# A hand-laid instruction order for attention plus feed-forward, with the list laid out anew: k of batch 0 loaded first, k of batch 1 behind v, 29 filler products

## Chip, core and metric

The kernel runs on one core of a Trainium2 chip. A core has TensorE (PE, which multiplies matrices), VectorE (DVE), ScalarE (ACT) and GpSimd (POOL) as computing engines, and SyncE (SP), which here only issues DMAs. Each engine runs its own list of instructions in order; semaphores make one list wait for another. The metric is the time of one execution on the device in microseconds (us); lower is better.

## The reference

Two parts, one behind the other. The first is block attention with sorted blocks: for 4 batches of 8 heads, 768 positions of 64 numbers are cut into 8 blocks of 96. A matrix `sort_net` of 8x8 per head is normalised five times over rows and columns, and the blocks of k and v are mixed by it.

```python
for _ in range(5):
    P = exp(P - max(P, axis=-1))
    P = P / sum(P, axis=-1)
    P = P / sum(P, axis=-2)
k_sorted = einsum('bhij,bhjcd->bhicd', P, k_blocks)
v_sorted = einsum('bhij,bhjcd->bhicd', P, v_blocks)
attn = softmax(scale * q_block @ k_sorted_block.T)
x = (attn @ v_sorted_block), heads side by side     # 3072 x 512
```

The second part is a feed-forward layer over the 3072 rows of x:

```python
h = x @ w_in                                        # 512 -> 2048
g = max(h, 0) + alpha * min(h, 0)
out = g @ w_out                                     # 2048 -> 512, float32
```

## The kernel before

The work goes by batch b (4) and within it by block (8), so by 32 groups g, each with the 8 heads of one block. For each group PE makes scores and softmax weights (products into the PSUM banks psS, psH), the products with v (psO, psYP), and transposes of the result into xT, which is the input of the feed-forward layer. That layer runs in chunks of groups: FFN1 (L875, w_in) writes psH, ACT and DVE turn psH into hT (L885, L889), FFN2 (L915, w_out) multiplies hT by w_out into psYP. The first chunks take 2 groups each, later ones 4.

Names that matter below:
- Loads. q, k and v of batch 0 come as three transfers of 768 KB, issued by POOL (L426 into hT, L449 into KS0 and VST0). The weights come in 4 (w_in, L960) and 2 (w_out, L965) transfers. Of the later batches k goes to KS1 and KS0 in turn (L449), v to VST1 and VST0 in two halves each (L465), q to QN, one transfer for each head (L431). All of these are issued on POOL's queue and their transfers land in the order of issue.
- `sinkhorn` (L548 to L562) is a chain of small steps on DVE and ACT; its last step gives Pb. PE spreads it over the partitions (L569), and DVE makes BDK from that (L573), the matrix that sorts k and v of batch 0.
- q of batch 0 is transposed by PE (L643) and copied into QTz0. k of batch 0 is sorted by PE (`prep_k`, L630) in six units and cast into KT0 by DVE or ACT (L401); one further copy, KT0<-KT0, fills a pad behind the first two units ("the pad copy"). v of batch 0 is copied into hT in eight units (hT<-VST, L401), sorted (L714) and copied into VS0.
- The matrices BDM and BDV, which sort k and v of batches 1 to 3, come from nine small PE products (L587, L590, "the spread"), two DVE products with mkj and mkjV and a sum dsel (L595, L600).
- For batches 1 to 3, KSz and VDz are padded copies of k and v (L655, L401) that PE multiplies (L668, L709).
- Scores are made twice: once turned, to find the row maximum nm (L759, L765), once for the exponentials (L781, L771). Group 1 is the first one. For g of 8 and more it is once (L756, nf).

What sets the order: nothing is planned at run time or at build time. `SEQ` (L32 to L79) is a table written as numbers. Each number is an operation of the program in the order in which `add` made it; a letter behind it picks the engine where there is a choice (p POOL, a ACT, d DVE; without a letter the first one allowed). `arrange` appends the operations to the five lists in the table's order, and `emit` puts a wait only where a list needs what another has made. An entry like `i15Y` stands for 15 filler products (L1047): identity times identity into a PSUM bank (Y is psYP, O psO, G psH), whose results nobody uses. PE runs them in its place in the list like all others. The kernel before has 42 of them: 22 ahead of the spread L569, 19 up to group 2's scores, one later.

Of the kernel before, what the change touches and what calls it, by code (L numbers as in the profile page):

```python
# [32 lines left out]
0 2 11 7 3 10 4 1 8 25 39 42 43 5 9 27 44 17 33 i1Y 45 i4Y 24 46 47 6 48 49 14 50 28 i2Y 51 52 53 i15Y 23 54  # L33
55 143 56 57 58 26 59 127 60 61 62 21 63 64 126 65 66 22 67 128 68 69 29 70 71 16 72 73 13 74 129 85 86 87 75
76 77 78 40 79 80 81 37 88 134 82 96 97d 94 91 92 98 38 89 130 12 144 95 90d i2Y 140 93a 83 84 100 i3Y 99d 20
136 101d 102d 105a 103d 154 i3Y 104 106 155 109 114 115 15 145 146 110 111 107d 112 113 i3Y 116 117d 147 108a
118 119d 148 122 123d 137 120 156 121 124 139 132 19 125d 135 233 133 157 i2Y 158 159 149 150 160d i3G 179 180
i1P 41 138 i2P 161 162d 151 152 18 181 30 35 36 34 153d 163 188 182 196 164 165 205 166 167p 197 189 190 191
232 206 183 230 184 207 192 193 185d 198 209 142 199 186 i1Y 231 237 210 141 194 195 221 208 131 187 213 200
211 212 222 244 214 201 223 215 216 248 245 224 249 202d 246 247 203 204d 250 251 217 225 258 218 236 226 262  # L40
263 219 220 234 241 235 227d 266 267 259 260 173 228 229 252 238 276 268 239 253 264 242 269 305 172 288d 170
174 240 280 261 279 286 243 270 315 265 289 290 277 278 271 287 293 294 306 307 272d 273 308 275 291 274 281
292 297 295 342 282d 298 283 309 284 296 301 302 285 316 343 317 310 299 344 300 328 311d 303 304 312 314 313d
320 326 332 32 321d 345 346 327 169p 333 324 329 347 325 353 348d 254 171p 349 334 335 175 354 255 256 350d
323 367 318 395 330 382 331 396 319d 392 336 351 393 383 384 397 394 419 416 420 322 352d 355 356 358d 31 365
398 399 337 366 357 338 408 421 409 359 257 425 417 400 418 426 422 339 428 360d 361 427 423 424 411 449 410
385 340 368 446 429 362 363 439 450 451 455 430 364d 447 448 369 176 458 459 414 443 456 415 386 387 388d 412
452 453 370 454 440 389 401 460 371 438 390d 402 476 488 457 479 413 403 404d 489 405 372 512 177 469 431 406d
432 477 178 441 461 480 444 478 482 442 481 485 433 434d 490 524 491 373 483 472 435 378 377 486 374 436 487
513 380 445 462 375 484 509 463 510 464d 470 379 471 506 507 381 511 465 466d 508 525 514 376 521 522 523 518  # L50
519 520 515 516d 526 527 492 517 474 545 475d 542 168 554 560 391 493 543 546 544 547 468 500 501 494d 555 548
473 561 549 550 502 437 495 496d 562 407 503d 551 552 556 499 577 553 563 578 579 498 504 505 533 528 529 557
558 589 530d 535 534 538 539 571 572 590 583 584 580 341 531 581 625 626 537 536 569 582 586 591 540 587 585
622 570d 541 573 574 575 532 600 576 627 588 623 631 598 624 599 564 632 559 628 629 565 601 634 566d 567 635
# [1035 lines left out]
```

## Time and profile before

| | us |
|---|---|
| median of 3 runs (lowest to highest) | 235.51 (235.39 to 235.55) |
| the profiled execution's own time | 235.32 |
| its span in the trace | 233.6 |
| DVE busy | 167.6 (72%) |
| ACT busy | 156.0 (67%) |
| POOL busy | 102.7 (44%) |

TensorE's granted clock is 1.00 in every stretch of the trace. Start times below are microseconds from the span's start; the own time of the execution is 1.7 us longer than its span.

How to read rows: in the timeline a row is a run of alike instructions: start, time from its first start to its last end, engine, line, operation, output<-input, size, count; in brackets idle time of that engine before it, and what ended it. In the windows view a row is a stretch of the span, with the busy time and count of PE, of PE's weight loads, of DVE, ACT and POOL, then the granted clock.

### The profile page before, as it was taken

The numbers are of one execution on the slowest core, as the hardware profiler recorded it, in microseconds if no ns is written. First come the engines' busy times: TensorE is split into PE (matmuls) and PEld (weight loads), VectorE is DVE, ScalarE is ACT, GpSimd is POOL, SyncE is SP. The second block draws the span as 40 slices with busy tenths as digits, with TensorE's granted clock in tenths as the row PEclk, the third lists the DMA queues.
The fourth block names the chain that finished last, engine by engine and source line by source line (L and its number), as shares of the span: only waits on it lengthen the run. The fifth ranks groups of instructions, "written<-read, shape, count | busy, mean of one in ns | idle before, by whom it ended". The sixth has DMA issues, their size and how long they took to land.

```text
span 233.6 us, 6277 instructions
## 1 busy us (share of the span) xinstructions
PE 225.4 (96%) x2528; PEld 140.4 (60%) x2556; DVE 167.6 (72%) x339; ACT 156.0 (67%) x417; POOL 102.7 (44%) x149
## 2 busy tenths in 40 slices
PE   6989999999999999999999999999999999999995
PEld 4356588795666666665566565555555555555653
DVE  5769799999878788586689668467787677544541
ACT  4187666989889678778888677766676674333431
POOL 7999139849049994863969953000000000000000
PEclk9999999999999999999999999999999999999999
DMA  5999999996996899869939997944643523410203
GB/s 66 220 206 204 218 200 185 186 182 99 218 189 106 115 152 174 196 102 225 192 63 164 137 103 164 154 90 79 130 107 74 112 51 109 124 45 0 94 0 135
DMA packets 73389, 31.36 MB, mean 134 GB/s; under 512 B 64512, under 2 KB 68368, under 8 KB 73360
## 3 DMA queue, kind: packets, MB, share of 16 engines
q0 software_dynamic: 24816, 13.63, 43.5%
q1 hardware_dynamic: 48544, 17.33, 37.2%
q8 instruction: 20, 0.33, 0.6%
q14 instruction: 9, 0.07, 0.1%
HBM read 27.28 MB, written 6.29 MB: 144 GB/s over the span
## 4 chain that ended last, share of the span: by engine, by line
PE 86%; DMA 4%; POOL 4%; DVE 3%; issue 2%; ACT 1%; POOLq 0%
PE psH L875 33%; PE psYP L915 28%; PE psYP L1047 4%; DMA VST<-in_v_dram 4%; PE psS L915 4%; PE psO L813 3%; PE psS L756 3%; POOL VDz L401 2%; PE psYP L668 2%; PE psYP L709 2%; PE psS L771 1%; PE psO L848 1%; DVE hT L401 1%; PE psS L781 1%; PE psO L915 1%
## 5 line engine op out<-in xcount | busy, mean ns | idle before, releaser
L889 DVE SCALAR_TENSOR_TENSOR hT<-t,omaT,psH 128x384 bf16<-128x384 f32 (+1 forms) x140 | 76.5, 568 | 37.4 <-ACT t L885 36.5
L875 PE MATMUL psH<-xT,w_in_bf 128*128 128x384 bf16 (+1 forms) x560 | 96.7, 310 | 0.6 <-DVE hT L889 0.6
L885 ACT ACTIVATE t<-psH 128x384 f32<-128x384 f32 x126 | 60.9, 493 | 44.5 <-PE psH L875 41.6
L915 PE MATMUL psYP<-w_out_bf,hT 128*128 128x512 bf16 x310 | 79.2, 379 | 1.4
L875 PEld LDWEIGHTS psH<-xT,w_in_bf 128*128 128x128 bf16 x560 | 50.0, 98 | 29.0 <-DVE hT L889 2.1
L915 PEld LDWEIGHTS psYP<-w_out_bf,hT 128*128 128x128 bf16 x336 | 30.8, 98 | 28.3 <-DVE hT L889 0.3
L793 ACT ACTIVATE Esb<-psS,nf 96x96 bf16<-96x96 f32 x192 | 46.1, 345 | 0.9 <-DVE nf L765 0.8
L401 POOL COPY VDz<-VST 64x384 bf16<-64x384 bf16 x40 | 34.5, 862 | 17.4 <-DMA VST<-in_v_dram 10.4
L655 POOL COPY KSz<-KS 64x512 bf16<-64x512 bf16 x36 | 22.0, 611 | 16.6 <-DMA KS<-in_k_dram 8.2
L765 DVE TENSOR_REDUCE nf<-psS 96x8 f32<-96x768 f32 x24 | 22.8, 950 | 6.4 <-PE psS L756 6.2
L826 DVE TENSOR_TENSOR xq<-psO,rec 96x512 bf16<-96x512 f32 x30 | 20.5, 684 | 0.7
L431 POOL DMA_DIRECT2D QN<-in_q_dram x24 | 19.9, 846 | 0.7 <-POOL QN L491 0.6
L401 ACT ACTIVATE outstg<-psYP 128x512 f32<-128x512 f32 x15 | 9.0, 601 | 7.7 <-PE psYP L915 7.5
L813 PEld LDWEIGHTS psO<-VS,ET 112*128 112x128 bf16 x248 | 11.1, 98 | 4.0 <-ACT xT L401 0.2
L1047 PE MATMUL psYP<-identb 128*128 128x512 bf16 x39 | 12.7, 470 | 0.8 <-ACT identb L401 0.8
L813 PE MATMUL psO<-VS,ET 112*128 112x65 bf16 x248 | 12.7, 194 | 0.0
L756 PEld LDWEIGHTS psS<-KT,QTz 128*128 128x128 bf16 (+1 forms) x192 | 10.7, 101 | 3.2 <-ACT KT L401 0.2
L401 ACT ACTIVATE VS<-psYP 112x512 bf16<-112x512 f32 x16 | 11.0, 688 | 2.1 <-PE psYP L714 1.1
L756 PE MATMUL psS<-KT,QTz 128*128 128x96 bf16 (+1 forms) x192 | 12.2, 207 | 0.0
L709 PEld LDWEIGHTS psYP<-BDV,VDz 128*128 128x128 bf16 x192 | 8.3, 98 | 3.0 <-POOL VDz L401 0.3
L401 ACT ACTIVATE KT<-psYP 128x512 bf16<-128x512 f32 x14 | 8.4, 600 | 2.2 <-PE psYP L668 2.0
L709 PE MATMUL psYP<-BDV,VDz 128*128 128x64 bf16 x192 | 9.5, 193 | 0.1
(140 smaller groups left out, 200.2 us busy)
## 6 DMA issues: line engine op xcount, KB each, us to landing
out_dram<-outstg SPq DMA_DIRECT2D x23, 256.0 KB, 2.5
KS<-in_k_dram POOLq DMA_DIRECT2D x3, 768.0 KB, 10.1
QN<-in_q_dram POOLq DMA_DIRECT2D x24, 96.0 KB, 4.5
w_in_bf<-in_moe_w_in_dram POOLq DMA_DIRECT2D x4, 512.0 KB, 16.8
w_out_bf<-in_moe_w_out_dram POOLq DMA_DIRECT2D x2, 1024.0 KB, 18.7
VST<-in_v_dram POOLq DMA_DIRECT2D x4, 384.0 KB, 11.1
hT<-in_q_dram POOLq DMA_DIRECT2D x1, 768.0 KB, 7.4
VST<-in_v_dram POOLq DMA_DIRECT2D x1, 768.0 KB, 12.8
```

Of the source, the lines that this page charges most:

```text
L401: return e.activation(o, i, ACTF.Copy) if e is nc.scalar else e.tensor_copy(o, i)
L655: G.add(POOL, lambda e, hp=hp: e.tensor_copy(AP(KSz, hp * 64 * 3072 + u % 3 * 1024 + hp * 64, [[3072, 64], [128, 8], [1, 64]]), AP(KS[n], ...
L709: inst = e.matmul(AP(t, off + dd * 64, [[row, 128], [1, 64]]), AP(VDz, (u % VSL * 8 + dd) * 128, [[VSL * 1024, 128], [1, 128]]), AP(BDV, b ...
L756: inst = e.matmul(o, AP(QTz[n], hp * 3072 + h4 * 768 + i * 96, [[6144, 128], [1, w]]), AP(KT[n], (h4 * 8 + i) * bk, [[ld, 128], [64, 2], [ ...
L765: G.add(DVE, lambda e: e.tensor_reduce(AP(nx, 0, [[8, 96], [4, 2], [1, 4]]), AP(psX, 0, [[1024, 96], [512, 2], [96, 4], [1, 96]]), AxisLis ...
L793: inst = e.activation(AP(Esb[me], p * 128, [[1024, 96], [64, 2], [1, 48]]), AP(psX, (p // 4) * 512 + (p % 4) * 96, [[1024, 96], [48, 2], [ ...
L813: inst = e.matmul(AP(psZ, hp * 512 + h4 * 68, [[1024, 128], [1, 65]]), AP(ET[me] if far else ET[m], pos(h4, hp) * 96, [[800, nk], [1, 128] ...
L875: inst = e.matmul(AP(pt, poff + x * n, [[1024, 128], [1, n]]), AP(w_in_bf, kt * DFF + (ft + x) * 128, [[KT_TILES * DFF, 128], [1, 128]]), ...
L885: G.add(ACT, lambda e: e.activation(AP(t1[tb], 0, [[384, 128], [1, k * n]]), AP(pt, poff, [[1024, 128], [1, k * n]]), ACTF.Relu, scale=-1. ...
L889: G.add(DVE, lambda e, x=x: e.scalar_tensor_tensor(out=AP(hT, (ft + x) * RING + tok % RING, [[FT_TILES * RING, 128], [1, n]]), in0=AP(t1[t ...
L915: inst = e.matmul(AP(bank[0], bank[1], [[1024, 128], [1, n]]), AP(hT, ft * RING + tok % RING, [[FT_TILES * RING, 128], [1, 128]]), AP(w_ou ...
L1047: inst = e.matmul(AP(t, off, [[1024, 128], [1, 512]]), identb[:, :], AP(identb, 0, [[128, 128], [0, 4], [1, 128]]))
```

## The change

Only `SEQ` differs; its text is one line shorter, so each line number behind it is one less in the changed kernel (L401 becomes L400, and so on). No operation other than fillers is added or removed. The first line of the table before and after:

```diff
-0 2 11 7 3 10 4 1 8 25 39 42 43 5 9 27 44 17 33 i1Y 45 i4Y 24 46 47 6 48 49 14 50 28 i2Y 51 52 53 i15Y 23 54
+0 10 1 7 5 2 3 8 39 4 42 43 44 45 12 11 35 46 47 48 49 6 50 16 51 40 13 52 9 27 53 i17Y 54 55 17 37 56 134 57
...
```

- Loads. POOL issued, with memsets between, q, k0, v0, half of v1, the four of w_in, k1, half of w_out, the other half of v1 and the eight QN transfers, the last five of these behind the hT copies. Now it issues k0, q, v0, k1, the four of w_in and one QN transfer, then makes its hT copies (which wait for v0), then issues half of w_out, a QN transfer, half of v1, and so on.
- Fillers. 29 instead of 42: 17 ahead of L569's spread, 8 ahead of group 1's scores, 4 behind the first product with v. The one after the first FFN1 groups and those between the scores and v's sorting are gone.
- FFN1 and FFN2. Eight FFN1 groups of 8 products (192 columns each) stand ahead of the first w_out product, where ten did.
- hT copies. POOL makes four and DVE two in a row (three and two before, and a third by DVE later); ACT makes the rest.

Three places are shown as rows of an engine's list.

The DVE list from BDK to the last step ahead of the first product with v (omaT is a small constant of the feed-forward layer, one0, mkj and mkjV masks), before:

```order
L573 TENSOR_TENSOR BDK<-mkh,psYP 128x128
L517 TENSOR_REDUCE one0<-identf 112x1
L401 CAST KT0<-psO 128x32x2x8
L401 CAST KT0<-psH 128x32x2x8
L401 CAST KT0<-psYP 128x32x2x8
L401 CAST KT0<-psH 128x32x2x8
L401 COPY hT<-VST0 128x8x48 x2
L765 TENSOR_REDUCE nm1<-psH 96x8
L765 TENSOR_REDUCE nm0<-psS 96x8
L401 COPY hT<-VST0 128x8x48
L401 CAST VS0<-psO 112x64x8 x4
L972 TENSOR_SCALAR omaT<-psYP 128x16
```

The same place of DVE's list after:

```order
L572 TENSOR_TENSOR BDK<-mkh,psYP 128x128
L505 TENSOR_REDUCE mkj<-identf 128x8
L400 COPY QTz0<-psO 128x768
L400 CAST KT0<-psYP 128x32x2x8
L400 CAST KT0<-psH 128x32x2x8
L400 CAST KT0<-psO 128x32x2x8
L400 COPY hT<-VST0 128x8x48 x2
L400 COPY KT0<-KT0 128x32x16
L764 TENSOR_REDUCE nm1<-psH 96x8
L400 CAST VS0<-psO 112x64x8
L764 TENSOR_REDUCE nm0<-psS 96x8
L400 CAST VS0<-psO 112x64x8
```

A copy of q into QTz0 has come from ACT to DVE and one cast of KT0 has gone to ACT; the pad copy KT0<-KT0 has come from ACT to DVE and stands behind the two hT copies, which wait for v0. Behind these rows DVE has one more cast of VS0 from psYP and one from psO, mkjV (which stood behind group 2's scores before) and omaT.

PE's list from the first product with v (L813, L812 after) to the third FFN1 group, before:

```order
L813 MATMUL psYP<-VS0,ET1 128x65 x8
L813 MATMUL psO<-VS0,ET0 128x65 x8
L1047 MATMUL psH<-identb 128x512 x3
L759 MATMUL psS<-KT0,QTz0 128x96 x8
L1047 MATMUL psYP<-identb 128x512 x3
L848 MATMUL psYP<-identb,xq1 128x96 x4
L848 MATMUL psO<-identb,xq0 128x96 x4
L781 MATMUL psS<-QTz0,KT0 128x96 x8
L771 MATMUL psS<-identb,nm0 128x96 x8
L587 MATMUL psYP<-Pb,selk 128x64 x3
L590 MATMUL psYP<-Pb,selk 64x64 x6
L875 MATMUL psH<-xT,w_in_bf 128x192 x8
```

After:

```order
L812 MATMUL psYP<-VS0,ET1 128x65 x8
L812 MATMUL psO<-VS0,ET0 128x65 x8
L1046 MATMUL psH<-identb 128x512 x4
L758 MATMUL psS<-KT0,QTz0 128x96 x8
L847 MATMUL psYP<-identb,xq1 128x96 x4
L847 MATMUL psO<-identb,xq0 128x96 x4
L780 MATMUL psS<-QTz0,KT0 128x96 x8
L770 MATMUL psS<-identb,nm0 128x96 x8
L874 MATMUL psH<-xT,w_in_bf 128x192 x8
L586 MATMUL psYP<-Pb,selk 128x64 x3
L589 MATMUL psYP<-Pb,selk 64x64 x6
```

The first FFN1 group has passed the nine products of the spread, and six fillers have become four.

POOL's list around the loads of batch 2 (KS0 and VST0 are free again by then), before:

```order
L401 COPY VDz<-VST1 64x8x48
L615 TENSOR_TENSOR BDV<-mkhV,dsel 128x64
L449 DMA KS0<-in_k_dram 128x3072
L401 COPY VDz<-VST1 64x8x48 x2
L504 MEMSET Esb1 96x16x16
L465 DMA VST0<-in_v_dram 64x3072 x2
L401 COPY VDz<-VST1 64x8x48
L401 COPY VDz<-VST0 64x8x48 x12
```

After:

```order
L400 COPY VDz<-VST1 64x8x48
L614 TENSOR_TENSOR BDV<-mkhV,dsel 128x64
L400 COPY VDz<-VST1 64x8x48 x3
L464 DMA VST0<-in_v_dram 64x3072
L400 COPY VDz<-VST1 64x8x48
L448 DMA KS0<-in_k_dram 128x3072
L464 DMA VST0<-in_v_dram 64x3072
L400 COPY VDz<-VST1 64x8x48 x2
L400 COPY VDz<-VST0 64x8x48 x4
```

The two halves of v2 and k2 are now issued behind the fifth and the sixth of POOL's VDz copies of batch 1; before, k2 was issued behind the fifth of eight and v2 behind the seventh.

More of the change, by code (lines that the diff above doesn't have):

```diff
@@ L32 @@
 SEQ = """
-0 2 11 7 3 10 4 1 8 25 39 42 43 5 9 27 44 17 33 i1Y 45 i4Y 24 46 47 6 48 49 14 50 28 i2Y 51 52 53 i15Y 23 54
[L34 to L52, printed above, removed]
```

70 lines of the change are left out of this document (44 added, 26 removed).

## The prediction, made before the changed kernel ran

> **What bounds the kernel now.** I read the page's head first.
>
> ```profile
> span 233.6 us, 6277 instructions
> ...
> PE 225.4 (96%) x2528; PEld 140.4 (60%) x2556; DVE 167.6 (72%) x339; ACT 156.0 (67%) x417; POOL 102.7 (44%) x149
> ```
>
> PE is busy for 96% of the span. But an average hides where the missing 8 us lie, so the second view is the table of stretches. I cut it at 28.7 us, where the first FFN1 group is about to start, and where the loads of batch 2 end.
>
> ```profile
> 28.70:54.80 26.10, 25.96 (x422) 21.21 (x423) 24.86 (x62) 20.78 (x37) 16.96 (x28) 1.00 1.40 178
> 54.80:73.00 18.20, 17.34 (x181) 10.88 (x182) 14.83 (x24) 15.96 (x49) 9.60 (x13) 1.00 0.99 178
> 73.00:92.00 19.00, 18.79 (x203) 12.09 (x206) 15.83 (x31) 14.66 (x44) 16.03 (x20) 1.00 1.15 132
> 92.00:231.00 139.00, 137.92 (x1108) 81.06 (x1123) 91.26 (x159) 88.19 (x254) 37.68 (x54) 1.00 0.61 111
> ```
>
> From 28.7 us on PE is full: 25.96 of 26.10, later 137.92 of 139.00. What a changed order can win there is only PE's waiting, most of it in the second row (0.86 us of 18.20). Ahead of 28.7 us PE runs fillers, and waits for loads and DVE. So the kernel is a **front** that ends when PE has enough to do, and a **body** with a fixed amount of PE work. The change does not touch that amount, apart from fillers. A microsecond in the front is a microsecond of the time, and so is each wait of PE in the body. DVE is the second engine to watch: 24.86 of 26.10 in the first stretch.
>
> The third view is the timeline of the front; the two rows in the last of these three fences are of the page's table of DMA issues (size, and us from issue to landing).
>
> ```profile
> 1.31 1.02 POOL L426 DMA_DIRECT2D hT<-in_q_dram  x1 [0.79 <-POOLq L1075]
> ...
> 4.12 0.55 POOL L449 DMA_DIRECT2D VST<-in_v_dram  x1
> ```
> ```profile
> 11.98 0.81 ACT L401 ACTIVATE QTz<-psO 128x768 bf16<-128x768 bf16 x1 [1.17 <-PE psO L643]
> ...
> 15.26 0.61 PE L1047 MATMUL psYP<-identb 128*128 128x512 bf16 x2
> ...
> 16.62 0.82 PE L1047 MATMUL psYP<-identb 128*128 128x512 bf16 x3
> ...
> 16.73 0.69 DVE L401 CAST KT<-psH 128x512 bf16<-128x512 f32 x1
> 17.08 3.09 POOL L401 COPY hT<-VST 128x384 bf16<-128x384 bf16 x3
> 17.34 2.10 DVE L401 COPY hT<-VST 128x384 bf16<-128x384 bf16 x2
> ...
> 17.61 0.35 PE L759 MATMUL psH<-KT,QTz 64*128 64x96 bf16 x8 [0.17 <-ACT QTz L401]
> ...
> 19.37 0.94 DVE L765 TENSOR_REDUCE nm<-psH 96x8 bf16<-96x768 f32 x1
> ...
> 21.10 0.58 DVE L401 COPY hT<-VST 128x384 bf16<-128x384 bf16 x1
> ...
> 25.00 0.42 PE L813 MATMUL psYP<-VS,ET 112*128 112x65 bf16 x8 [0.17 <-DVE omaT L972]
> ...
> 27.86 0.34 DVE L401 COPY xT<-psYP 128x384 bf16<-128x384 bf16 x1
> ...
> 28.33 0.37 DVE L509 TENSOR_REDUCE mkjV<-identf 128x8 f32<-128x128 f32 x1
> ```
> ```profile
> hT<-in_q_dram POOLq DMA_DIRECT2D x1, 768.0 KB, 7.4
> ...
> VST<-in_v_dram POOLq DMA_DIRECT2D x1, 768.0 KB, 12.8
> ```
>
> q lands at 1.31 + 7.4 = 8.7 us, v of batch 0 at 4.12 + 12.8 = 16.9. k lies between them, and the three are equally large, so one of them takes about 4.1 us and the second lands near 12.8. Group 1's scores (L759, 17.61) are early enough; DVE reaches the maximum nm only at 19.37, when its two hT copies are done. From nm to the first product with v (L813) it is 25.00 - 19.37 = 5.63 us of VS casts, exponentials and omaT.
>
> **The change part by part.** The sum is made against the profiled execution's own 235.32 us, 0.19 below the median shown (235.51); I carry the sum over as it is.
>
> Fillers: 13 fewer. Two take 0.61 us and three 0.82, so one more costs 0.21; were they on the path, 13 would be worth 13 x 0.21 = -2.7 us. I take 0, since what they stand in front of waits for transfers and DVE anyway: they fill time, and take it only where the awaited thing is there already. The granted clock is 1.00 in all stretches, and no run shows here what it would be with fewer.
>
> Front: k first, q second. q's transposes and copies move from 8.7 to behind 12.8; sorted k waits for BDK from the sinkhorn chain as before. The step that decides is DVE's list, by the rows quoted: a copy of q into QTz0 is now DVE's (ACT's took 0.81), then three casts of 0.69, then the two hT copies (2.10), then the **pad copy**, and only then can L759 run, since it reads KT0 with its pad. So: q at 12.8, transposes of 36 products (about 1 us) and waits, QTz copy 14.25 to 15.1; casts to 17.15; v has landed at 16.9, so nothing waits for it; hT copies to 19.25; pad copy to 20.05; L759's 0.35 to 20.4, and nm starts there. Before it started at 19.37: +1.03. Behind nm a DVE hT copy is gone (-0.58) and mkjV has come in (+0.37). The first product with v moves by 1.03 - 0.58 + 0.37 = **+0.8**, to about 25.8.
>
> The pad copy on DVE is in no row of before. Its nearest rows: a copy of the same kind of data alone, 0.34 (27.86); the hT copies of DVE beside POOL's, 2.10 / 2 = 1.05 against 0.58 alone (21.10), so +0.47 for the company. POOL will be in the midst of its four hT copies (1.03 each by the row at 17.08), so I take 0.34 + 0.47 = 0.8; with the largest surcharge of a row (+0.72, below) it is 1.06. The ends of this term: pad copy 0.34 and hT copies at 0.58 each give -0.6; 1.06 gives +1.1.
>
> Spread behind the first FFN1 group: PE's first useful FFN work is earlier by the nine small products, but DVE gets its two L595 products and dsel behind them later, while it is nearly full (24.86 of 26.10, so 1.24 idle). Lower end 0, if the idle time covers it; upper end +1.1, if nearly all that idle time opens anew in front. DVE's list loses work in this stretch to ACT (a KT1 cast, a VDz copy of 0.57, BDV), which speaks for the lower half: I take **+0.4**.
>
> Batch 2's loads earlier, and VDz copies moved: the two waits of PE in the body.
>
> ```profile
> 54.65 1.29 DVE L401 COPY VDz<-VST 64x384 bf16<-64x384 bf16 x1
> ...
> 57.63 1.47 PE L875 MATMUL psH<-xT,w_in_bf 128*128 128x384 bf16 x8 [0.57 <-DVE hT L889]
> ...
> 58.73 0.57 DVE L401 COPY VDz<-VST 64x384 bf16<-64x384 bf16 x1
> ```
> ```profile
> 66.99 10.88 POOL L401 COPY VDz<-VST 64x384 bf16<-64x384 bf16 x12 [8.11 <-DMA VST<-in_v_dram]
> ```
> ```profile
> 54.81 0.50 PE L756 MATMUL psS<-KT,QTz 128*128 128x96 bf16 x8
> 55.15 0.81 PE L875 MATMUL psH<-xT,w_in_bf 128*128 128x384 bf16 x4
> ```
> ```profile
> 68.12 0.52 PE L756 MATMUL psS<-KT,QTz 128*96 128x96 bf16 x8
> 68.77 0.41 PE L709 MATMUL psYP<-BDV,VDz 128*128 128x64 bf16 x8
> ```
>
> At 57.63 PE has stood for 0.57 us because DVE was late with hT, and DVE was late because a VDz copy beside POOL's copies took 1.29 instead of 0.57 (+0.72); that copy now stands earlier in DVE's list. At 68.12 a run of L756 keeps PE 0.65 us to the next start instead of 55.15 - 54.81 = 0.34, because L709 needs VDz of batch 2, whose data landed shortly before 66.99: POOL had stood 8.11 us for it. Its loads are now issued behind the fifth and sixth copy instead of the seventh, and the KSz and VDz copies themselves stand earlier, so the landing comes some microseconds sooner and 0.31 goes. Together **-0.9**. Lower end of the gain: 0, if another wait follows in each place; what is late next is the scores' exponentials on ACT, which was 15.96 of 18.20 busy.
>
> Sum: 235.32 + 0.8 + 0.4 - 0.9 = 235.6 us, rounded to the tenth. With all ends added up: 235.32 - 0.6 - 0.9 = 233.8, and 235.32 + 1.1 + 1.1 = 237.5.
>
> Here a rule bears on the pad copy. The Trainium skill, "SBUF — State Buffer", section "Who interferes with whom", says that DVE in a 2-port mode and GpSimd share one pair of ports as an exclusive lock, held for the whole instruction, and that the other fully blocks. By that rule alone each DVE copy would wait out a POOL copy; 1.03 + 0.58 = 1.61 instead of the 1.05 that the row at 17.34 has, so this trace shows less than a full block there, and 1.29 against 0.57 at 54.65 shows one nearer to it. What the full block would do to the pad copy is the first rival below.
>
> **The rivals.** *Slower, the pad copy late (0.21).* DVE's pad copy may be held back by POOL's row of four hT copies, one longer than before. Held for one whole copy it ends at 19.25 + 1.03 + 0.34 = 20.6 instead of 20.05 (+0.6: 236.2); held until the last, at about 17.0 + 4 x 1.03 + 0.34 = 21.5 (+1.4: 237.0). The middle is 236.6. It decides from an end of 20.4 on. For it: 1.29 against 0.57 in one place. Against: 1.05 in the very place of the hT copies. This is the mechanism that the page's rule names; its price here comes from the rows.
>
> *Slower, w_out late (0.12).* Half of w_out is now issued behind POOL's hT copies and stands in front of less other work on PE.
>
> ```profile
> L965 POOL DMA_DIRECT2D w_out_bf<-in_moe_w_out_dram x2: 886/912/937, 12.3 to 39.2; - x2
> ...
> DMA to landing us min/median/max: 11.4/18.7/26.0
> ```
> ```profile
> 40.35 0.81 PE L915 MATMUL psYP<-w_out_bf,hT 128*128 128x512 bf16 x3
> ```
>
> Before, it was issued at 12.3 and landed 26.0 later, at 38.3; the first use was near 40.35. Now it is behind one half of v1 less (384 KB) and one QN transfer more (96 KB), so 288 KB / 768 KB x 4.1 = 1.5 us earlier, 36.8. But two FFN1 groups of about 0.8 us fewer stand ahead of its first use, so that comes at about 38.7. If the landing is later than estimated by 1.9 us, each further microsecond costs one: with one such it is 236.6.
>
> *Faster, the front no later (0.29).* If q lands nearer to 11 than 12.8, or the hT copies need less beside POOL, the first product with v comes at 25.2 or earlier, and DVE's shorter list in the body gives back the 0.4: 235.32 - 0.9 - 0.3 = 234.1. Against it is that the pad copy is an addition to DVE's list at the place where nm waits. That the change gives no room for late landings at all, since PE waits for q and v as before, is not a case of its own: its time is the forecast's.
>
> **How the numbers follow.** The forecast, with its neighbourhood, has 0.38, the faster rival 0.29, the two slower ones 0.33 together. The range of 234.1 to 237.0 leaves out about 1 in 10 on each side. About 0.2% (0.47 us) is what a measurement of this kernel can tell from no change: 235.04 to 235.98 of the median is the same, so the forecast's case counts as the same, the first and second rival as slower, the third as faster.
>
> **What would show it.** In the changed profile: q's landing near 12.8 by the first QTz copy; the pad copy of DVE beginning near 19.2 and taking about 0.8; nm of group 1 near 20.4 and the first L812 near 25.8; no wait of PE at the third L709 of batch 1, and POOL's first VDz copy of batch 2 earlier than 66; the first w_out product not waiting for a transfer. Wrong would be a front at 25 or less (then faster), a pad copy beginning late or taking over 1.1, or a wait of PE in the stretch from 28.7 to 54.8 over 0.5 us.

## The result

| | before | after |
|---|---|---|
| median, us (lowest to highest, runs) | 235.45 (234.77 to 235.55, 6 runs) | 237.43 (236.85 to 238.01, 6 runs) |
| ratio to before, 95% interval | | 1.009 (1.0066 to 1.0114) |
| own time of the profiled execution, us | 235.32 | 237.79 |

The changed kernel is slower by about 2 us; 235.6 was forecast, and 237.0 was the upper end of the range. The head of the profile after:

```profile
span 236.1 us, 6278 instructions
...
PE 223.5 (95%) x2543; PEld 139.1 (59%) x2543; DVE 165.1 (70%) x339; ACT 157.5 (67%) x425; POOL 101.8 (43%) x148
```

The same stretches as in the prediction, after (length, then PE, PEld, DVE, ACT, POOL, clock, DMA share, GB/s):

```profile
28.70:54.80 26.10, 24.69 (x416) 20.49 (x413) 22.00 (x57) 20.79 (x38) 14.91 (x24) 1.00 1.37 181
54.80:73.00 18.20, 17.53 (x173) 10.49 (x172) 13.71 (x26) 15.16 (x44) 8.27 (x12) 1.00 1.00 164
73.00:92.00 19.00, 18.70 (x194) 11.52 (x193) 15.40 (x28) 13.84 (x46) 18.28 (x24) 1.00 1.06 119
92.00:231.00 139.00, 139.00 (x1146) 81.06 (x1143) 92.97 (x165) 91.11 (x264) 36.37 (x53) 1.00 0.60 111
```

The first row carries most of the loss: PE is busy for 24.69 us of 26.10, where it was 25.96. Behind 92 us nothing is lost. The clock is 1.00 throughout, so the loss is waiting.

To date the loss I counted off PE's products other than fillers in each trace, by the time they take when nothing waits (the same sum in every kernel), and noted when PE had done how much. Differences to the profile before, in us (plus is later, good to about 0.15 us); the last five columns are of experiments told below:

```
work done  before at | after | front only  cut at 38  cut at 48  vdz_on_dve | v_before_k
   12        26.53   | -0.10 |   0.67        0.01      -0.58      -0.29     |   0.79
   20        35.93   |  0.07 |   0.67       -0.15      -0.74      -0.46     |   0.80
   22        38.04   |  0.45 |   0.67        1.15       1.53       0.50     |   0.80
   28        44.37   |  0.49 |   0.63        1.12       1.56       0.54     |   0.76
   30        46.60   |  0.94 |   0.65        1.15       2.18       1.01     |   0.80
   36        52.94   |  1.89 |   0.60        1.09       2.99       1.26     |   0.74
   38        54.89   |  1.94 |   0.65        1.14       3.07       2.48     |   0.80
   40        57.62   |  1.22 |   0.66        1.16       2.50       1.75     |   0.31
   48        65.64   |  1.67 |   0.66        1.16       2.65       2.05     |   0.47
   56        73.99   |  2.46 |   0.36        0.85       2.34       1.75     |   0.17
  100       118.12   |  2.47 |   0.33        0.83       2.32       1.77     |   0.14
```

After the change PE is level at 36 us, 0.45 late at the first w_out product (38 us), 1.9 late at 55 us; there it gets 0.7 back (before's own wait at 57.63 is gone), and by 74 us it is 2.5 late. These are PE's waits in the timeline after (start, us, line, operands, count; in brackets idle time and releaser):

```profile
46.63 0.41 PE L812 MATMUL psO<-VS,ET 112*128 112x65 bf16 x8
47.50 0.41 PE L667 MATMUL psYP<-BDM,KSz 128*128 128x64 bf16 x8 [0.46 <-ACT KT L400]
...
51.68 0.40 PE L708 MATMUL psYP<-BDV,VDz 128*128 128x64 bf16 x8
52.71 0.42 PE L812 MATMUL psO<-VS,ET 112*128 112x65 bf16 x8 [0.63 <-DVE xT L400]
52.97 0.82 PE L874 MATMUL psH<-xT,w_in_bf 128*128 128x192 bf16 x8
53.95 0.41 PE L708 MATMUL psYP<-BDV,VDz 128*128 128x64 bf16 x8 [0.16 <-ACT VS L400]
...
60.83 0.51 PE L755 MATMUL psS<-KT,QTz 128*128 128x96 bf16 x8 [0.21 <-ACT Esb L792]
...
69.75 0.40 PE L812 MATMUL psO<-VS,ET 112*128 112x65 bf16 x8 [0.46 <-DMA ET<-Esb]
...
75.15 0.41 PE L708 MATMUL psYP<-BDV,VDz 128*128 128x64 bf16 x8 [0.30 <-POOL VDz L400]
```

By starts a wait is a little longer than its bracket: L708 at 51.68 and its successor are 1.03 apart, where two such runs follow each other in 0.24 (55.23, 55.47), so 0.79 is lost. Counted like this the six cost 0.63, 0.79, 0.32, 0.39, 0.61 and 0.46 us: 3.2 in all, in place of the two of before (0.73 by starts, and 0.31).

What ACT did ahead of the first three:

```profile
45.20 0.87 ACT L400 ACTIVATE VDz<-VST 64x384 bf16<-64x384 bf16 x1
46.08 0.87 ACT L884 ACTIVATE t<-psH 128x384 f32<-128x384 f32 x2
46.84 0.60 ACT L400 ACTIVATE KT<-psYP 128x512 bf16<-128x512 f32 x1
...
50.25 0.86 ACT L400 ACTIVATE VDz<-VST 64x384 bf16<-64x384 bf16 x1
51.12 0.49 ACT L884 ACTIVATE t<-psH 128x384 f32<-128x384 f32 x1
...
52.34 0.87 ACT L400 ACTIVATE VDz<-VST 64x384 bf16<-64x384 bf16 x1
53.22 0.68 ACT L400 ACTIVATE VS<-psYP 112x512 bf16<-112x512 f32 x1
```

Each late cast (KT, VS) stands directly behind other work, without a gap. The second wait, for xT, comes from ACT by way of DVE:

```profile
51.65 0.74 DVE L888 SCALAR_TENSOR_TENSOR hT<-t,omaT,psH 128x192 bf16<-128x192 f32 x2 [0.27 <-ACT t L884]
```

DVE's xT copy (52.30) stands behind these two hT steps, which waited for ACT's t of 51.12, and t stood behind the VDz copy of 50.25. The windows view cut around these waits, after and then before:

```profile
43.50:49.00 5.50, 5.04 (x100) 4.36 (x99) 4.97 (x14) 5.43 (x10) 4.80 (x8) 1.00 1.42 204
...
51.00:54.50 3.50, 2.71 (x46) 2.24 (x45) 2.38 (x7) 3.45 (x7) 0.07 (x1) 1.00 0.90 182
```
```profile
43.50:49.00 5.50, 5.47 (x101) 4.65 (x102) 5.13 (x12) 5.24 (x10) 4.17 (x6) 1.00 1.37 202
...
51.00:54.50 3.50, 3.45 (x45) 2.29 (x43) 3.28 (x9) 3.24 (x6) 2.96 (x6) 1.00 1.08 135
```

Where PE waits, ACT is busy for 5.43 of 5.50 and 3.45 of 3.50 us, while DVE has 2.38 of 3.50 in the second and POOL nothing. In the average of the whole stretch ACT is at 20.79 of 26.10, which looks idle enough. But in the kernel before, ACT has 5.24 and 3.24 in the same windows, hardly less, and PE hardly waits. So a full ACT alone does not make the waits: what counts is what stands ahead of each cast in its list.

POOL's list around batch 2's loads, after:

```profile
54.43 0.85 POOL L400 COPY VDz<-VST 64x384 bf16<-64x384 bf16 x1 [5.67 <-PE psYP L708]
55.23 0.59 POOL L464 DMA_DIRECT2D VST<-in_v_dram  x1
...
56.60 0.57 POOL L448 DMA_DIRECT2D KS<-in_k_dram  x1
57.18 0.53 POOL L464 DMA_DIRECT2D VST<-in_v_dram  x1
...
69.08 3.54 POOL L400 COPY VDz<-VST 64x384 bf16<-64x384 bf16 x4 [9.62 <-DMA VST<-in_v_dram]
```

The loads moved ahead by a row or two in the list, but the copy that they stand behind waited 5.67 us for PE. So the first half of v2 is issued at 55.23 (56.97 before) and the second at 57.18, now with k2 in front of it. VDz of batch 2 starts at 69.08 instead of 66.99, later rather than sooner. The ET transpose of the wait at 69.75 and the VDz of the wait at 75.15 both come behind that landing.

The front after, on DVE and PE, and the first use of w_out (the second fence is the trace's answer for w_out's line):

```profile
13.35 0.96 DVE L400 COPY QTz<-psO 128x768 bf16<-128x768 bf16 x1 [0.31 <-PE psO L642]
...
16.07 1.64 DVE L400 COPY hT<-VST 128x384 bf16<-128x384 bf16 x2
17.62 0.95 DVE L400 COPY KT<-KT 128x512 bf16<-128x512 bf16 x1
19.10 0.95 DVE L764 TENSOR_REDUCE nm<-psH 96x8 bf16<-96x768 f32 x1 [0.53 <-PE psH L758]
...
24.90 0.42 PE L812 MATMUL psYP<-VS,ET 112*128 112x65 bf16 x8 [0.75 <-DVE omaT L971]
...
38.06 0.55 PEld L914 LDWEIGHTS psYP<-w_out_bf,hT 128*128 128x128 bf16 x4 [0.15 <-DMA w_out_bf<-in_moe_w_out_dram]
```
```profile
L964 POOL DMA_DIRECT2D w_out_bf<-in_moe_w_out_dram x2: 892/895/898, 21.7 to 34.4; - x2
...
DMA to landing us min/median/max: 16.3/16.6/16.9
```

nm comes at 19.10 and the first product with v at 24.90, where 20.4 and 25.8 were forecast; before had 19.37 and 25.00. w_out's first half landed 16.3 us behind its issue at 21.7, at 38.0, and PE uses it at 38.06: no slack at all.

### The profile page after: what moved, and what is told of

Same layout as the page of the kernel before. It is cut to its first block, busy times and chain, and to the rows that moved or that the text cites. A ratio compares the mean times of both kernels' runs of the same rounds, so it can differ in the third digit from the quotient of the medians.

```text
span 236.1 us, 6278 instructions
## 1 busy us (share of the span) xinstructions
PE 223.5 (95%) x2543; PEld 139.1 (59%) x2543; DVE 165.1 (70%) x339; ACT 157.5 (67%) x425; POOL 101.8 (43%) x148
## 4 chain that ended last, share of the span: by engine, by line
PE 75%; DVE 8%; ACT 7%; DMA 4%; POOL 2%; issue 2%; POOLq 0%
PE psH L874 30%; PE psYP L914 27%; DMA ET<-Esb 4%; PE psS L914 4%; PE psS L755 3%; PE psO L812 3%; PE psYP L667 2%; PE psYP L708 2%; POOL VDz L400 1%; ACT VDz L400 1%; DVE hT L888 1%; ACT t L884 1%; DVE KT L400 1%; ACT VS L400 1%; PE psO L847 1%
## 5 line engine op out<-in xcount | busy, mean ns | idle before, releaser
L914 PE MATMUL psYP<-w_out_bf,hT 128*128 128x512 bf16 x336 | 84.1, 379 | 0.0
L914 PEld LDWEIGHTS psYP<-w_out_bf,hT 128*128 128x128 bf16 x336 | 30.7, 98 | 28.0 <-DMA w_out_bf<-in_moe_w_out_dram 0.2
L400 POOL COPY VDz<-VST 64x384 bf16<-64x384 bf16 x40 | 33.9, 848 | 18.2 <-DMA VST<-in_v_dram 9.6
L764 DVE TENSOR_REDUCE nf<-psS 96x8 f32<-96x768 f32 x24 | 22.8, 950 | 7.3 <-PE psS L755 7.0
L825 DVE TENSOR_TENSOR xq<-psO,rec 96x512 bf16<-96x512 f32 x29 | 19.8, 683 | 0.4
L812 PE MATMUL psO<-VS,ET 112*128 112x65 bf16 x248 | 12.7, 194 | 1.1 <-DVE xT L400 0.6
L812 PEld LDWEIGHTS psO<-VS,ET 112*128 112x128 bf16 x248 | 11.0, 98 | 4.6 <-DVE hT L888 0.9
L400 ACT ACTIVATE KT<-psYP 128x512 bf16<-128x512 f32 x16 | 9.6, 599 | 2.5 <-PE psYP L667 2.3
L708 PEld LDWEIGHTS psYP<-BDV,VDz 128*128 128x128 bf16 x192 | 8.4, 98 | 4.0 <-POOL VDz L400 0.7
L400 ACT ACTIVATE VS<-psYP 112x512 bf16<-112x512 f32 x14 | 9.6, 687 | 1.3 <-PE psYP L708 0.9
L400 ACT ACTIVATE outstg<-psYP 128x512 f32<-128x512 f32 x13 | 7.8, 597 | 3.9 <-PE psYP L914 3.9
L708 PE MATMUL psYP<-BDV,VDz 128*128 128x64 bf16 x192 | 9.5, 193 | 0.5 <-POOL VDz L400 0.3
L914 PE MATMUL psS<-w_out_bf,hT 128*128 128x512 bf16 (+1 forms) x48 | 9.8, 344 | 0.0
```

The costliest lines, as they stand in the source:

```text
L400: return e.activation(o, i, ACTF.Copy) if e is nc.scalar else e.tensor_copy(o, i)
L708: inst = e.matmul(AP(t, off + dd * 64, [[row, 128], [1, 64]]), AP(VDz, (u % VSL * 8 + dd) * 128, [[VSL * 1024, 128], [1, 128]]), AP(BDV, b ...
L764: G.add(DVE, lambda e: e.tensor_reduce(AP(nx, 0, [[8, 96], [4, 2], [1, 4]]), AP(psX, 0, [[1024, 96], [512, 2], [96, 4], [1, 96]]), AxisLis ...
L812: inst = e.matmul(AP(psZ, hp * 512 + h4 * 68, [[1024, 128], [1, 65]]), AP(ET[me] if far else ET[m], pos(h4, hp) * 96, [[800, nk], [1, 128] ...
L914: inst = e.matmul(AP(bank[0], bank[1], [[1024, 128], [1, n]]), AP(hT, ft * RING + tok % RING, [[FT_TILES * RING, 128], [1, 128]]), AP(w_ou ...
```

## The experiments

My theory A was that the body's new order loses the time (engines late in turn), the rival B that the front and the w_out landing do. All kernels below compute the whole reference. Beside them the kernel before had medians of 235.08 to 235.32; each ratio is to its runs on the same chip at the same time.

### Where: lists joined from both kernels

The five lists of one kernel up to a point, those of the other behind it; what the first part lacks is added in the second's order. As an example PE's list of the second kernel at its joint, against after:

```diff
-L874 MATMUL psH<-xT,w_in_bf 128x192 x8
 L586 MATMUL psYP<-Pb,selk 128x64 x3
 L589 MATMUL psYP<-Pb,selk 64x64 x6
+L874 MATMUL psH<-xT,w_in_bf 128x192 x8
```

Before's lists up to the spread, then after's:

> The lists of before up to the spread of BDM (28.7 us), the lists of the changed kernel from there on. Theory A (the loss lies in the body, in the waits of PE between 44 and 75 us that the new lists make): 237.0 to 237.4, about as slow as the changed kernel. Theory B (the loss comes from the front: the new order of the first loads and what lands late because of it): 235.3 to 235.8.

Measured 240.08 (239.75 to 240.44), 1.020 (1.0185 to 1.0215). After's lists up to the first FFN1 group, then before's:

> The reverse: the lists of the changed kernel up to its first FFN1 group (28.9 us), with its load order, 29 fillers and DVE's pad copy, then the lists of before. Theory A: 235.4 to 235.8, since the first FFN1 group starts 0.15 us later by the two traces. Theory B: 237.0 to 237.4. My forecast's own term for the front, +0.8, would give 236.2 or 236.3.

Measured 235.79 (234.96 to 237.43), 1.0026 (1.0003 to 1.005). After's lists up to 56 us, then before's:

> The changed lists up to the first 384-column FFN1 group (56.3 us), then the lists of before. By the two traces PE has lost about 1.6 us against before up to there, and 0.8 behind it. Theory A: 236.8 to 237.2, if the waits between 44 and 56 us come from these lists. If it is the later loads of batch 2 and what waits for them (rival C): 235.5 to 236.0.

Measured 238.05 (237.66 to 239.09), 1.0121 (1.0093 to 1.0148). After's lists up to the first w_out product (38 us), and up to the FFN1 group at 47.7 us:

> The changed lists up to its first w_out product (38.1 us; spread, load order and front included), then the lists of before, which put two FFN1 groups ahead of that product. If the stretch up to 38 us costs nothing but through w_out's landing: 235.3 to 235.9, as the cut at 28.9 us gave (235.79). If the spread behind the first FFN1 group costs its +0.4 there: 236.1 to 236.4.

> The changed lists up to the FFN1 group at 47.7 us, then the lists of before. By the work done on PE the changed kernel's profile is behind before by 0.1 us at 36, 0.5 at 38.5, 0.9 at 47.5 and 1.9 at 54.8. If these losses stay where they arise: 236.2 to 236.6 here, between 235.79 (cut at 28.9) and 238.05 (cut at 56.3). If the loss comes all at once with the lists from 48 to 56 us: 235.5 to 236.0; if all of it with those up to 48: 237.2 to 238.0.

Measured 236.72 (236.29 to 238.1), 1.0074 (1.005 to 1.0099), and 237.65 (236.34 to 238.43), 1.0101 (1.0069 to 1.0132).

After's front alone costs about 0.3% (0.03 to 0.5). The more of after's body a kernel has, the slower it is: 235.79, 236.72, 237.65, 238.05. The table above shows it inside the traces: "front only" and "cut at 38" lose nothing behind their joint, "cut at 48" still loses 1.5 between work 28 and 38. The first kernel, with before's front, has after's waits in its trace (for KT 0.5, xT 0.6, VS 0.2, Esb 0.2) and loses about 1.4 between work 28 and 38. That is theory A.

The sizes show less than the places. 240.08, 238.05 and 236.72 lie above all that was expected of them, and the traces show other losses too: the first kernel is already 0.97 late at 23 us, ahead of its joint, the third waits 1.71 us for VDz of batch 2 at 72.30, behind its own, and "cut at 38" goes from -0.15 to 1.15 at its joint.

### The front and w_out

The pad copy given to ACT, in after and in the front-only kernel:

```diff
-DVE: L400 COPY KT<-KT 128x32x16
+ACT: L400 ACTIVATE KT<-KT 128x32x16      (behind ACT's second KT cast)
```

> The changed kernel with the pad copy of KT0 on ACT, behind its second KT cast, as in before. My forecast made that copy the step that delays nm and with it the front, +0.8: 236.6 to 236.8 without it. If something else ends the front's chain (the VS casts, exponentials and omaT), or PE then waits for w_out at 38: 237.2 to 237.6.

> The lists of the changed kernel up to its first FFN1 group, with the pad copy on ACT, then those of before, where two more FFN1 groups stand ahead of the first w_out product. If the front's gain of about 1 us by the pad copy on ACT is real and only the landing of w_out ate it: 234.6 to 235.0, against 235.79 of the same kernel with the pad copy on DVE. If not: 235.4 to 236.0.

Measured 238.06 (237.35 to 238.61), 1.0118 (1.0096 to 1.014), and 235.75 (234.98 to 236.73), 1.0023 (0.9998 to 1.0047). In the first the FFN1 groups come 1.0 us earlier (27.85 instead of 28.86), and all of that is lost at the first w_out product, as its weight loads show:

```profile
38.58 0.55 PEld L914 LDWEIGHTS psYP<-w_out_bf,hT 128*128 128x128 bf16 x4 [1.68 <-DMA w_out_bf<-in_moe_w_out_dram]
```

That the 1.0 us come from the pad copy is not shown: with the same front the first FFN1 group starts at 28.81 in gate_moved, told below, and after's own front gave anything from 28.04 to 29.10 in eight traces.

w_out's first half issued ahead of the QN memset, right behind w_in (11.23 us instead of 21.68):

```diff
 L959 DMA w_in_bf<-in_moe_w_in_dram 128x2x1024 x3
+L964 DMA w_out_bf<-in_moe_w_out_dram 128x8x512
 L490 MEMSET QN 128x6x64
```

> The changed kernel with w_out's first half issued right behind w_in, ahead of the hT copies. Its landing was 38.0 in the changed kernel's profile and 38.5 to 39.2 in three related runs, against a first use at 38.1. If that landing decides in some executions: the times fall to the lower of the two groups that the changed kernel showed, 236.8 to 237.0, and spread less. If not: 237.2 to 237.8.

Measured 237.24 (237.1 to 237.5), 1.0086 (1.0071 to 1.0101); it landed at 37.46. The pad copy on ACT and the first w_out product behind the next FFN1 group:

```diff
-L914 MATMUL psYP<-w_out_bf,hT 128x512 x4
 L847 MATMUL psO<-identb,xq 128x96 x4
 L758 MATMUL psS<-KT,QTz 128x96 x8
 L667 MATMUL psYP<-BDM,KSz 128x64 x8
 L874 MATMUL psH<-xT,w_in_bf 128x192 x8
+L914 MATMUL psYP<-w_out_bf,hT 128x512 x4
```

> The run with the pad copy on ACT had its first FFN1 group 1.0 us earlier than the changed kernel and lost it all before the first w_out product, which waited for the landing at 38.5. Here it is the same kernel with that product behind the transposes of group 3, one score run, one k unit and one FFN1 group. If the landing of w_out was the gate: 236.3 to 236.9, that is at least 0.9 under the 238.06 of the run with the pad copy on ACT. If not: 237.4 to 238.2.

Measured 238.4 (237.75 to 239.01), 1.0124 (1.0076 to 1.0172): the product now waits for nothing, but PE does at 39.77 for a KT cast of ACT (0.63). The spread ahead of the first FFN1 group, dsel directly behind its products:

```diff
-L874 MATMUL psH<-xT,w_in_bf 128x192 x8
 L586 MATMUL psYP<-Pb,selk 128x64 x3
 L589 MATMUL psYP<-Pb,selk 64x64 x6
+L874 MATMUL psH<-xT,w_in_bf 128x192 x8
```

> The changed kernel with the nine spread products ahead of the first FFN1 group again, and the sum dsel directly behind the two products on DVE instead of at 36.3 us. My forecast put +0.4 on that move. If the three waits of 0.2 us at 36.2, 37.0 and 39.7 us come from dsel's place: 236.7 to 237.0. If PE then only waits longer for w_out's first half, which lands at 38.0: 237.2 to 237.6.

Measured 237.09 (236.82 to 237.66), 1.0081 (1.0061 to 1.0101). By work 22 it is as late as after (0.46 against 0.45), but by another way:

```profile
36.94 0.83 PE L874 MATMUL psH<-xT,w_in_bf 128*128 128x192 bf16 x8
38.19 0.81 PE L914 MATMUL psYP<-w_out_bf,hT 128*128 128x512 bf16 x3 [0.42 <-DMA w_out_bf<-in_moe_w_out_dram]
```

The last FFN1 group ahead of the w_out product starts at 36.94, where after has 37.30, and then PE waits 0.42 for w_out. With w_out early it is the reverse: PE doesn't wait for w_out, and loses about 0.4 between work 20 and 22 as in after. The kernel that has both edits (all four remedies, below) loses only about 0.2 there, and its w_out product starts at 37.27. So in these traces, one of each kernel, the spread's new place costs 0.3 to 0.4, and w_out's landing hides that when only one of the two is put back.

In the kernels with after's lists here w_out landed between 36.3 and 39.1. Where it landed at 38.3 or later (five profiles), PE was 0.87 to 1.53 late at work 22, even where it had been up to 0.9 early before. So this wait for w_out is a real gate, and it takes what the front gains; at 38.0, as in after's own profile, it costs next to nothing. w_out early narrowed the times to 0.4 us (four executions; 1.16 in after), but its median is lower by only 0.2, so the gate isn't the main loss.

### ACT's and DVE's lists between 43 and 58 us

A KT cast and a VS cast of batch 1 from ACT to DVE:

```diff
-ACT: L400 ACTIVATE KT<-psYP 128x32x2x8
-ACT: L400 ACTIVATE VS<-psYP 112x64x8
+DVE: L400 CAST KT<-psYP 128x32x2x8        (behind the xT copy at 45.80)
+DVE: L400 CAST VS<-psYP 112x64x8          (behind the xT copy at 52.30)
```

> The changed kernel with two of the evictions that stand on ACT in it given to DVE: the cast of KT1 for k unit 4 of batch 1, and the cast of VS1 for v unit 1. Theory A1 (the changed lists load ACT where PE waits for it next): the waits behind 46.6 and 53.0 us go (0.63 and 0.32 by the trace), 236.4 to 236.7. Rival A2 (DVE has no room there either, or PE meets the next wait): 237.1 to 237.6.

Measured 237.67 (237.23 to 238.06), 1.0102 (1.0086 to 1.0119). The wait at 47.50 is gone, and one for DVE stands behind it; the second row is DVE's:

```profile
48.54 0.83 PE L874 MATMUL psH<-xT,w_in_bf 128*128 128x192 bf16 x8 [0.96 <-DVE hT L888]
```
```profile
47.47 0.70 DVE L604 TENSOR_TENSOR BDM<-mkhM,dsel 128x64 bf16<-128x64 f32 x1
```

Two of ACT's VDz copies moved behind the KT and VS casts that were late (a third moved two places forward, which the rows don't show, as they leave out the units):

```diff
-L400 ACTIVATE VDz<-VST 64x8x48
 L884 ACTIVATE t<-psH 128x384 x2
 L400 ACTIVATE KT<-psYP 128x32x2x8
+L400 ACTIVATE VDz<-VST 64x8x48
...
+L400 ACTIVATE VS<-psYP 112x64x8
 L400 ACTIVATE VDz<-VST 64x8x48
-L400 ACTIVATE VS<-psYP 112x64x8
```

> The changed kernel with three VDz copies of ACT moved in ACT's own list: that of v unit 1 behind the KT1 cast of k unit 4, that of unit 2 two places forward, that of unit 4 behind the VS1 cast of unit 1. Theory A3 (ACT's VDz copies, 0.87 us each, stand where PE waits for ACT's next result): the waits behind 46.6 and 53.0 us go or shrink, 236.4 to 236.8. Rival A2 (DVE is the next to be late in each place, as it was in the run with two casts on DVE): 237.1 to 237.7.

Measured 237.23 (236.38 to 238.59), 1.0093 (1.0065 to 1.012). The casts are in time, and the exponentials behind the moved copy are late:

```profile
48.03 0.35 PE L758 MATMUL psS<-KT,QTz 64*128 64x96 bf16 x8 [0.65 <-ACT ET L803]
```

Two of ACT's VDz copies around 50 to 53 us given to DVE, which is the least busy there:

```diff
 DVE: L400 COPY xT<-psO 128x4x96
+DVE: L400 COPY VDz<-VST 64x8x48
 DVE: L820 RECIPROCAL rec<-psO 96x8
 DVE: L825 TENSOR_TENSOR xq<-psO,rec 96x512
+DVE: L400 COPY VDz<-VST 64x8x48
 DVE: L400 CAST VS<-psYP 112x64x8
-ACT: L400 ACTIVATE VDz<-VST 64x8x48 x2
```

> The changed kernel with ACT's two VDz copies of units 2 and 4 of batch 1 given to DVE. If ACT being full between 51.0 and 54.5 us (3.45 of 3.50 busy, DVE 2.38) makes PE's waits of 0.80 us at 51.7 and 0.32 us at 53.0, the two shrink by about 0.5 us together: 236.8 to 237.0 us. If the next engine is late in its place, as in the two runs before that moved single copies: 237.2 to 237.7 us.

Measured 237.87 (237.6 to 238.27), 1.0118 (1.01 to 1.0136). Its PE and DVE rows:

```profile
52.42 0.42 PE L812 MATMUL psO<-VS,ET 112*128 112x65 bf16 x8 [0.28 <-DVE xT L400]
...
55.76 0.41 PE L708 MATMUL psYP<-BDV,VDz 128*128 128x64 bf16 x8 [0.99 <-DVE VS L400]
```
```profile
53.92 1.08 DVE L400 COPY VDz<-VST 64x384 bf16<-64x384 bf16 x1
55.01 0.70 DVE L400 CAST VS<-psYP 112x512 bf16<-112x512 f32 x1
```

The two waits do shrink: between work 30 and 36 PE's lateness grows by 0.95 in after (0.94 to 1.89), here by 0.25 (1.01 to 1.26). That is 0.7 us, somewhat more than the 0.5 expected of ACT's being full. By work 38 another 1.2 us is lost, as DVE's second copy took 1.08 and put off the VS cast behind it. So what ACT has ahead of those casts does make the waits, and taking it away gains nothing as the lists stand: another wait takes its place, in all three kernels.

### Batch 2's loads

In after, all three loads ahead of the copy that waits for PE:

```diff
-L400 COPY VDz<-VST 64x8x48 x3
+L400 COPY VDz<-VST 64x8x48 x2
 L464 DMA VST<-in_v_dram 64x3072
-L400 COPY VDz<-VST 64x8x48
 L448 DMA KS<-in_k_dram 128x3072
 L464 DMA VST<-in_v_dram 64x3072
-L400 COPY VDz<-VST 64x8x48 x2
+L400 COPY VDz<-VST 64x8x48 x4
```

> The changed kernel with one edit: the three loads of batch 2 (v2 in two halves, k2) stand ahead of POOL's fifth VDz copy of batch 1, which waits for PE, so they are issued near 48.8 instead of 55.2 to 57.2 us. If the waits at 69.75 (L812 for ET, 0.46 to 0.6 us) and 75.15 (L708 for VDz, 0.3 to 0.47 us) come from v2's late landing (68.9): 236.2 to 236.6, and both waits gone. If something else follows there, or the earlier transfers get in the way of QTz's: 237.2 to 237.8.

Measured 237.25 (236.87 to 237.93), 1.0074 (1.0056 to 1.0092). v2 landed at 61.91 instead of 68.88, and the waits at 69.75 and 75.15 are gone from its trace; its w_out landed at 38.66, and PE was 0.65 us later than in after at work 22, which takes back more than half. So those two waits come from v2's late loads. They are not in every execution of after's loads: PE waits for VDz in the four traces where v2 landed at 68.88 or later, and in none of the five where it landed at 68.03 or earlier. The same loads early in before, alone, and with DVE's VDz copy of 54.65 given to ACT besides, in exchange for one that DVE makes behind nf and two hT:

```diff
-L401 COPY VDz<-VST 64x8x48 x3
+L401 COPY VDz<-VST 64x8x48 x2
+L465 DMA VST<-in_v_dram 64x3072
+L449 DMA KS<-in_k_dram 128x3072
+L465 DMA VST<-in_v_dram 64x3072
+L401 COPY VDz<-VST 64x8x48
...
-L449 DMA KS<-in_k_dram 128x3072
 L401 COPY VDz<-VST 64x8x48 x2
 L504 MEMSET Esb 96x16x16
-L465 DMA VST<-in_v_dram 64x3072 x2
```

> Before with only the three loads of batch 2 issued early, no VDz copy moved. The wait of 0.31 at 68.1 us should go: 234.9 to 235.1. If the early transfers get in the way of the QTz transposes, or if they are the cause of the six executions of 245 us and more of the run with both edits: 235.4 and over, or times of 245 again.

> Before, with nothing but the forecast's third term done in its own lists: the three loads of batch 2 stand ahead of POOL's fourth-last VDz copy of batch 1 (issued near 48 instead of 54 to 57.5 us), and the VDz copy that DVE made at 54.65 goes to ACT in exchange for another that DVE makes at 58. My forecast's -0.9 for those two waits gives 234.3 to 234.6. If other waits take their place, as they did in the changed kernel: 235.0 to 235.6.

Measured 234.65 (ten of eleven from 234.37 to 235.2, one 251.73), 0.998 (0.9961 to 0.9999); and 0.9999 (0.997 to 1.0028), where five of ten executions took 245 to 251 us and the ratio is that of the others. Such a long execution was traced where four of the remedies stood together in after (w_out early, spread first, VDz moved, loads early); those of the two kernels above were not:

> The changed kernel with the single edits together: w_out's first half behind w_in, the spread ahead of the first FFN1 group, batch 2's loads early, three VDz copies moved on ACT. Each alone moved the median by 0.2 to 0.35. If the waits are separate, they add up: 236.2 to 236.6. If PE meets the next late engine in each place: 236.9 to 237.4.

Measured 246.08 (244.1 to 251.65), 1.0449 (1.0391 to 1.0507). Its PE, and two stretches of the windows view:

```profile
67.73 0.80 PE L755 MATMUL psS<-KT,QTz 128*128 128x96 bf16 x8 [7.67 <-DMA QTz<-QN]
```
```profile
63.00:66.00 3.00, 0.00 (x0) 0.00 (x0) 0.00 (x0) 0.00 (x0) 0.00 (x0) 0.56 1.00 154
66.00:69.00 3.00, 1.27 (x10) 0.92 (x11) 0.43 (x1) 0.00 (x0) 1.08 (x2) 0.50 1.19 172
```

The loads were issued from 47.85 on. A transpose of QTz issued at 46.68, which landed within 8 us in before, landed at 67.60, with the last of the loads; PE stood 7.67 us and then ran at half clock. So in the last experiment v2's loads come sooner than in before, but behind the landing of the third of these transposes (54.4): v2 and k2 are exchanged in before:

```diff
-L449 DMA KS<-in_k_dram 128x3072
+L465 DMA VST<-in_v_dram 64x3072 x2
 L401 COPY VDz<-VST 64x8x48 x2
 L504 MEMSET Esb 96x16x16
-L465 DMA VST<-in_v_dram 64x3072 x2
+L449 DMA KS<-in_k_dram 128x3072
```

> The kernel before with the loads of k and v of batch 2 exchanged in POOL's list: v at k's place, which was behind the landing of the third transpose of q, k at v's old place. If what cost the executions at 245 us and more was that v's transfers were issued ahead of that transpose's landing, none shows up here, and the 0.31 us wait of 68.12 us goes: 234.9 to 235.1 us. If v's early landing is worth nothing, because k is then as late: 235.3 to 235.5 us. Executions at 245 us again would say that it was not the transposes' place.

Measured 234.58 (234.06 to 235.48, 12 executions), 0.9975 (0.9961 to 0.999). POOL's rows and two stretches of the windows view:

```profile
54.84 1.13 POOL L465 DMA_DIRECT2D VST<-in_v_dram  x2
...
62.36 3.59 POOL L401 COPY VDz<-VST 64x384 bf16<-64x384 bf16 x4 [2.77 <-DMA VST<-in_v_dram]
```
```profile
28.70:54.80 26.10, 26.08 (x438) 21.28 (x435) 24.77 (x65) 20.23 (x37) 16.15 (x26) 1.00 1.40 177
54.80:73.00 18.20, 18.12 (x186) 11.29 (x185) 15.21 (x26) 16.57 (x50) 12.33 (x17) 1.00 0.98 175
```

VDz of batch 2 starts 4.6 us sooner than before (62.36, 66.99), PE has no wait left (18.12 of 18.20), none of the twelve executions is long, and it beats both kernels, before by 0.25% (0.1 to 0.4). In the table it loses 0.8 in a late front of that one execution and gains 0.66 in the body (0.80 to 0.14). Most of that is a surprise: 0.49 of it is before's wait at 57.63, nearly gone too, as DVE's VDz copy took 0.80 here instead of 1.29 (POOL's next copy began half a microsecond behind it, at 55.96; in before it began at 54.69, 0.04 behind). In the trace of the loads early in before the copy took 0.75 and that wait is gone as well.

## Why the prediction was wrong

**Body waits, -0.9: the step that failed.** That PE's two waits of before would go was right, and worth 0.7 at the first place. "0, if another wait follows in each place" was to be the worst of it, and that is what happened and more: six waits of 3.2 us in other places. The end of the term was set at the two waits that I had looked at, as if a new order could only remove waits. It also read ACT's load from an average of the stretch, and not what stands ahead of each hand-over in ACT's list. The prediction's own sign of being wrong, a wait of over 0.5 us ahead of 54.8, is the one at 52.71 (0.63). The three kernels with single copies moved show that the waits hang on ACT and DVE in turn. In the sum's terms after's profile has about 0 for the front, 0.45 between 36 and 38 us, and 3.2 less 1.0 for the body: 2.6, where the count gives 2.5.

**"DVE's list loses work in this stretch to ACT", taken as a gain.** No gain came of it: DVE went from 24.86 to 22.00 us in the first stretch, but four of PE's six new waits come from ACT (KT, VS and Esb directly, xT by way of DVE), and for three of them a VDz copy of ACT of 0.86 or 0.87 stands ahead (45.20, 50.25, 52.34). ACT's own sum hardly changed (20.78 and 20.79); it is the place of its work that did.

**V2's loads "some microseconds sooner".** Wrong: 69.08 instead of 66.99. The step went by places in the order and left out that the copy ahead of them waits for PE, and that k2 now stands ahead of v2's second half. (The sign "third L709 of batch 1" names the wrong product: the L709 at 68.77 is the first of batch 2.) v2_loads_first shows its price in after's profile, the waits of 0.61 and 0.46.

**Front, +0.8.** About 0: nm 19.10, first product with v 24.90. q landed at 12.4, DVE's QTz copy began at 13.35 instead of 14.25, and the hT copies took 0.82 each instead of 1.05. The pad copy was near its upper bound (0.95 against 0.8, and 1.06 as the end). The front-only kernel is 0.3% slower with an interval that begins at 0.03%, and the same lists differ by 0.8 to 1.1 us in their front from one execution to the next (before's in v_before_k, 0.79 late; after's in eight traces, 28.04 to 29.10). So one profile can't settle this term closer, and it isn't where the 2 us are.

**Spread, +0.4.** About right, by one trace each: 0.36 up to the last FFN1 group ahead of w_out in spread_first, and about 0.4 between work 20 and 22 with w_out early. The medians don't settle it: that of spread_first is 0.34 lower, with ranges that overlap. And taken back alone it gains nothing at work 22, since w_out isn't there sooner.

**Fillers, 0.** Nothing speaks against it: PE was level with before at 36 us with 13 fewer.

**The rivals.** The pad copy was late only within its bounds. By the Trainium skill, "SBUF — State Buffer", section "Who interferes with whom", whichever of DVE (in a 2-port mode) and GpSimd issues first gets the shared ports for its whole instruction, and the other blocks. The traces agree: the pad copy took 0.95 at 17.62, when a POOL copy was under way from 17.39 to 18.42, so it waited out the rest of that. In two_back_on_dve, with the same lists there, DVE's copies came first; its pad copy took 0.29, and POOL's first hT copy took 1.79 where 0.85 is the median of its four:

```profile
17.60 0.29 DVE L400 COPY KT<-KT 128x512 bf16<-128x512 bf16 x1
```

The 1.05 that the prediction held against the rule is a mean that hides this: 0.99 and 1.18 for the two copies in before, 0.54 and 1.18 in after. The w_out rival had the right place and direction: it lands at 38.0 to 39.1, not 36.8, and its 1.9 us of slack was none. But it decides only in some executions, and it is the smaller part of the loss. The two together explain why a range with an upper end of 237.0 was too low: no case had more than one new wait in it.

**What stays open.** Which order of ACT's and DVE's lists between 38 and 55 us would take away the 1.5 us there isn't found; three moves only shifted the waits. No kernel had all of the body's remedies with v2 behind the transposes.

## What to carry to other kernels

Where PE is full at 96%, a new order of all lists can hardly gain what PE doesn't wait for, and can lose anywhere: look at what stands ahead of each hand-over in its engine's list, in windows of a few microseconds, and not at the engine's load over a stage. A load "earlier in the list" is earlier only if what stands ahead of it doesn't wait. And a single exchange whose effect can be followed (v2 ahead of k2) was worth more here than the whole list laid out anew.

## What the runs showed of the hardware

- A DMA transpose is slow beside loads. The third transpose of QTz landed 11.4 to 11.8 us behind its issue where the three loads stood ahead of it (v2_on_before, t4_on_before, v2_loads_first), and 4.6 to 5.0 us in before, after and v_before_k. In all_fixes one that was issued ahead of the loads (46.68, landing 67.60) took 20.9 us with all three in flight. What decides that is open: with the loads early, one execution in eleven, five in ten, none in four and five in five took over 244 us.
- The granted clock fell to 0.5 while PE stood still from 60.1 to 67.7, and four products L914 behind it took 1.9 us instead of 1.03. The Trainium skill, "TensorE: Matmul & The Clock Gate", section "What's actually happening", has half the clock after an idle window of some 3.4 us; 0.56 as the mean of 63 to 66 agrees.
- BDM on DVE took 0.70 us beside POOL's copies (two_back_on_dve) where it took 0.22 in after. The pad copy on DVE took 0.29 to 0.31 in three traces and 0.93 to 0.95 in nine.
- w_out's first half, issued between 21.7 and 22.8 us, landed anywhere from 37.4 (vdz_moved) to 39.2 (the front-only kernel), and later issue doesn't explain it: 22.75 gave 39.24, and 22.76 gave 38.32 (two_back_on_dve).
